# Filter rows and normed rows turned by DMA instead of TensorE in a fused SSM-convolution and SwiGLU kernel

## The chip, the cores and the metric

The kernel runs on one core of a Trainium2 chip. Its engines work in parallel: TensorE (PE, matrix products and transposes into PSUM), VectorE (DVE), ScalarE (ACT), GpSimd (POOL) and SyncE (SP), which issues nearly all DMAs. The metric is device time in microseconds of a whole execution; a kernel's figure is the median of several runs.

## The reference

The inputs are a sequence of S = 2048 rows with D = 576 columns, in bf16. Two residual branches follow each other, each behind a layer norm whose scale and shift come from a condition vector.

```python
mod = (silu(c) @ w_mod).reshape(1, 6, 1, -1)     # sa, ca, ga, sb, cb, gb
h = layernorm(x) * (1 + ca) + sa                 # x is A_q
# branch A: a short convolution of k by 4 taps, times v -> kv;
# then a long causal convolution along the sequence, by FFT of length 2S, with the filters ssm_k [D, S]
y = irfft(rfft(kv) * rfft(ssm_k).T)[:S] + kv * ssm_D
x = x + ga * (h * y)
# branch B: SwiGLU, w1 and w3 [576, 4608], w2 [4608, 576]
h = layernorm(x) * (1 + cb) + sb
x = x + gb * ((silu(h @ w1) * (h @ w3)) @ w2)
```

What matters below: the filters lie in DRAM with the channel as the row (ssm_k is [D, S]), while the convolution wants time on the partitions; and the normed rows of branch B have time on the partitions, while the products with w1 and w3 want the channel there. Both need a transpose.

## The kernel before, in words

**Tiling.** The sequence is cut into 8 blocks of B = 256 rows. A block is held as [128 partitions, 2, 576], where partition p holds rows 2p and 2p + 1. Branch A works block by block: the long convolution is done with the spectra of short blocks. For block s the filter's spectrum W (w_spectrum) gives V[s] (v_block), the spectrum of kv gives X[s] (x_spectrum), and the result of block s is the inverse of the sum of products X[i]·V[s - i] (pair, lines 412 to 425: VectorE's long products). X and V of earlier blocks are partly spilled to DRAM (keep_x, keep_v) and read back (get, line 442).

Branch B works on row blocks of RB = 512 rows, two convolution blocks each: stream(r) makes h3 = silu(h w1)·(h w3) for 36 column tiles of F, and down(r) multiplies it by w2, in two halves of 288 columns with nine chunks of w2 each. The last row block has its own stream_halves. w1 and w3 arrive in jobs of four column tiles (load_w13) in three buffers wst; in down the third of these holds a ring of four w2 chunks (NW2 = 4).

**Who makes whom wait.** While row block r goes through TensorE, the convolution of blocks 2r + 2 and 2r + 3 is computed beside it. conv(s0) is a generator of steps with a cost in microseconds at each yield. stream and down call advance after each piece of their own work, and advance runs steps until their costs have caught up (CONV_US, rate). So the convolution's TensorE work lies between the products of branch B, in an order fixed when the program is written out. end() runs all steps that are left. The instructions of each engine's queue are then ordered by a planner, which goes by dependencies and by its own estimate of when they are ready; `behind(engine)` pins the next instructions behind the last one written for that engine, and issue_after behind a named one. SP's queue is such a queue too: an instruction that waits there holds back all that follow.

**The filter rows.** load_k(s) (line 290) brings ssm_k[:, 256 s : 256 s + 256] into knat as five tiles of 128 channels by 256 times. k_rows(s) (line 368) transposes them on TensorE: ten transposes of 128x128 (line 376), five for the even and five for the odd times, into one PSUM buffer; ScalarE copies it to kT (line 378), the [128, 2, 576] form that w_spectrum multiplies (line 329). PSUM has four buffers of two banks for everything, one of which is taken here.

**The normed rows.** outcome(s) finishes a block: inverse (line 555), residual, then the statistics of the second norm on ScalarE (ln_sums, line 452), a few small VectorE and GpSimd instructions (ln_var, ln_shift), and the normed rows h2row, one buffer of [128, 2, 640], in which columns 512 to 576 stand twice (normed_act, line 582). turn_all(s) (line 794) turns h2row on TensorE with ten transposes (line 587), and `turned` (line 609) copies the result out of PSUM on ScalarE with scale and shift (1 + cb, sb) applied: five instructions of 128x256 (line 617) into h2T, of which there are two, one for each parity of the row block. For the even block of a pair turn_all is called inside the outcome of the odd block (`between`). For the odd block 2r + 3 it is called in down(r), in the second half behind chunk 7 of w2 (line 1088); chunk 8 follows, and then the first products of row block r + 1 (lines 967, or 1031 in the last row block) read h2T.

Block 0 and block 1 come first (first_block, conv_second), with row block 0 started on half of its rows.

Of the kernel before, what the change touches and what calls it, by code (L numbers as in the profile page):

```python
# [37 lines left out]
EPS = 1e-5  # L38

# [7 lines left out]
class _Kernel:  # L47
    def __init__(self, ctx, tc, q, k, v, shift_k, ssm_k, ssm_D, w1, w3, w2, c, w_mod, out):
        self.tc, self.nc = tc, tc.nc
        self.q, self.k, self.v = q, k, v  # L50
        self.shift_k, self.ssm_k, self.ssm_D = shift_k, ssm_k, ssm_D
        self.w1, self.w3, self.w2, self.c, self.w_mod, self.out = w1, w3, w2, c, w_mod, out
        pool = lambda name, **kw: ctx.enter_context(tc.tile_pool(name=name, **kw))
        self.const = pool("const", bufs=1)
        self.psum = pool("psum", bufs=4, space=bass.MemoryType.PSUM)
        self.dram = pool("spill", bufs=1, space=bass.MemoryType.DRAM)
        self.spec = pool("spec", bufs=4)
        self.wprev = pool("wprev", bufs=2)
        self.prod = pool("prod", bufs=1)
        self.acc = pool("acc", bufs=1)  # L60
        self.ld = pool("ld", bufs=1)
        self.kvp = pool("kvp", bufs=1)
        self.x1p = pool("x1p", bufs=4)
        self.lnp = pool("lnp", bufs=1)
        self.small = pool("small", bufs=4)
        self.hp = pool("hp", bufs=3)
        self.xo, self.hg, self.accs, self.l1 = {}, {}, {}, {}
        self.X, self.V, self.Wl = {}, {}, {}
        self.w13, self.kept = {}, {}

# [225 lines left out]

    def load_x(self, s):
        t = self.x1p.tile([P, 2, D], BF16, name="x1", tag="x1")
        self.nc.sync.dma_start(t[:], self.q[B * s:B * (s + 1), :].rearrange("(p c) d -> p c d", c=2))
        self.xo[s] = t  # L300
# [67 lines left out]
    def k_rows(self, s):  # L368
# [10 lines left out]
        if 2 < s < NBLK - 1:  # L379
            self.load_k(s + 1)  # L380
# [61 lines left out]
    def get(self, which, i):  # L442
        t = self.spec.tile([P, 6, D], BF16, name=which, tag=which, bufs=3 if which == "X" else 4)
        src = self.Xd if which == "X" else self.Vd
        self.nc.sync.dma_start(t[:].rearrange("p a d -> p (a d)"), src[i])
# [306 lines left out]
    def outcome(self, s, fill, waits, between=None, quick=False):  # L752


        def steps():
# [19 lines left out]
            else:  # L775
# [5 lines left out]
                yield -waits[2] / 2  # L781
                stats = self.ln_var(*sums, "l2")
# [11 lines left out]
    def turn_all(self, s):  # L794

        pt = self.ps((P, 2, 1024), BF16)
        for cc in range(2):
            self.turn(pt, cc)
        self.turned(s, pt, 0, 2)

    def conv_second(self):
        yield from self.gate_stats(1)
# [9 lines left out]
        self.load_k(2)  # L812
        yield from self.x_sums(1)
        yield from self.pair(self.X[1], self.V[0], 1)
# [4 lines left out]
    def conv(self, s0):  # L819
        s1 = s0 + 1  # L820
        if s0 == 2:
            self.load_k(s1)
# [4 lines left out]
        def filters():  # L827
            yield from self.k_rows(s1)
# [33 lines left out]
        def beside():  # L862
# [7 lines left out]
            yield from self.gate_stats(s1)  # L870
            if s0 > 2:
                yield from self.pair(X0, self.V[s0], s0)
# [5 lines left out]
            yield from self.pair(X0, self.V[s1], s1)  # L878
            self.gate_var(s1)
# [19 lines left out]
        if s1 + 1 < NBLK:  # L899
            with self.behind(self.nc.sync):  # L900
                self.load_kv(s1 + 1)
        yield from self.gate(s1)
        ahead = self.mix(self.filter_ahead(s1 + 1)) if s1 + 1 < NBLK else ()
        yield from self.outcome(s1, ahead, (5.0, 4.5, 5.0, 0.0), lambda: self.turn_all(s0))

    def filter_ahead(self, s):
        yield from self.k_rows(s)
        yield -4.0
        yield from self.w_spectrum(s)

# [156 lines left out]
    def down(self, r, rate):  # L1067
        nc = self.nc
        for h in range(2):
# [4 lines left out]
            for f0 in range(0, NF, W2C):  # L1074
# [3 lines left out]
                last = f0 + W2C == NF  # L1078
                order = [(f, t) for f in range(W2C) for t in range(4)]
# [8 lines left out]
                if h == 1 and f0 // W2C == 7 and r + 1 < NRB:  # L1088

                    self.end()  # L1090
                    self.turn_all(2 * r + 3)
                if (f0 // W2C) % 4 == 3:
# [132 lines left out]
```

## Time and profile before

| | us |
|---|---|
| median of 8 runs | 515.68 (514.29 to 516.08) |
| the profiled execution | 515.95 |
| its span in the trace | 514.2 |
| TensorE busy | 495.8 |
| VectorE busy | 337.5 |
| ScalarE busy | 294.7 |
| GpSimd busy | 27.1 |

The stages lie about so: the first block up to 35 us; row block 0 with blocks 1 to 3 up to 165, its down from 125; row block 1 up to 285, its down from 245; row block 2 up to 403, its down from 365; row block 3 to the end, its down from 474. TensorE's granted clock averages 0.993 over the span.

A row of a group reads: line, engine, operation, what it writes and reads, shape and count, then busy time, the mean of one in ns, and the idle time of the engine just before these instructions with what ended it. A row of a timeline begins with its start and its duration in us. A row of a window gives, for each engine, busy time and number of instructions, and at the end the granted clock, the mean busy share of the 16 DMA engines and GB/s.

### The profile page before, as it was taken

How to read it: one execution, taken by the hardware profiler on the slowest of the kernel's cores; microseconds unless marked ns; L12 is line 12 of the kernel's file. 1: busy time of each engine (PE TensorE's matmuls, PEld its weight loads, DVE VectorE, ACT ScalarE, POOL GpSimd, SP SyncE). 2: the span in 40 equal slices, each digit the busy share in tenths (PEclk: the TensorE clock that was granted, in tenths of full speed). 3: DMA queues.
4: the chain of work that ended last, by engine and by line, in shares of the span. 5: the costliest groups of instructions: out<-in, count | busy, mean ns of one | idle time of the engine just before them, and what ended most of it. 6: DMA issues, size and time to landing. Idle time of an engine off the chain costs nothing.

```text
span 514.2 us, 9042 instructions
## 1 busy us (share of the span) xinstructions
PE 495.8 (96%) x3630; PEld 299.8 (58%) x3650; DVE 337.5 (66%) x438; ACT 294.7 (57%) x581; POOL 27.1 (5%) x43
## 2 busy tenths in 40 slices
PE   6999999999999999999999999999999999999996
PEld 3667865457777444443787443434678555555774
DVE  8789899899889375999389995289761212112012
ACT  5749779769155679579352565975804555555000
POOL 4200001000001000000001000000000000000000
PEclk9979999999999999999999999999999999999999
DMA  8967869659989875387789594545554453460562
GB/s 259 285 205 208 278 205 300 189 180 320 323 274 324 277 217 170 104 293 270 210 266 290 166 321 155 171 108 170 160 143 113 149 174 113 165 183 3 139 169 62
DMA packets 101597, 104.25 MB, mean 203 GB/s; under 512 B 4979, under 2 KB 94132, under 8 KB 101556
## 3 DMA queue, kind: packets, MB, share of 16 engines
q1 hardware_dynamic: 101534, 103.68, 65.5%
q8 instruction: 28, 0.46, 0.4%
q14 instruction: 13, 0.11, 0.1%
q10 hardware_dynamic: 22, 0.01, 0.0%
HBM read 94.23 MB, written 9.44 MB: 202 GB/s over the span
## 4 chain that ended last, share of the span: by engine, by line
PE 67%; DVE 19%; DMA 4%; ACT 4%; issue 2%; POOL 2%; POOLq 0%; SPq 0%; DVEq 0%; ACTq 0%
PE ps L967 26%; PE ps L1085 16%; PE ps L1031 14%; DVE p L422 4%; PE ps L978 4%; DVE z L424 4%; DMA h<-in_w_mod_dram 2%; DMA kh<-in_A_k_dram 2%; PE ps L555 2%; PE ps L329 2%; DVE og L1107 1%; DVE h L992 1%; PE ps L315 1%; DVE kv L349 1%; POOL l2r L464 1%
## 5 line engine op out<-in xcount | busy, mean ns | idle before, releaser
L967 PE MATMUL ps<-h2T,wst 128*128 128x512 bf16 (+1 forms) x1037 | 198.9, 340 | 1.5 <-issue 0.3
L967 PEld LDWEIGHTS <-wst 128*128 128x128 bf16 x1056 | 100.0, 98 | 85.9 <-issue 14.6
L1085 PE MATMUL ps<-wst,h 128*128 128x288 bf16 x1152 | 146.0, 286 | 2.5 <-DMA wst<-in_B_w_dram 1.7
L1085 PEld LDWEIGHTS <-h 128*128 128x128 bf16 x1152 | 112.1, 98 | 32.7 <-issue 3.8
L985 ACT ACTIVATE h<-ps 128x512 bf16<-128x512 f32 x108 | 64.8, 600 | 63.3 <-PE ps L978 35.0
L1031 PE MATMUL ps<-h2T,wst 64*128 64x512 bf16 x648 | 70.3, 376 | 0.5 <-ACT h2T L617 0.5
L989 ACT CAST u<-ps 128x512 bf16<-128x512 f32 x108 | 63.3, 586 | 0.0
L1031 PEld LDWEIGHTS <-wst 64*128 64x128 bf16 x648 | 36.1, 94 | 34.1 <-issue 0.7
L422 DVE TENSOR_TENSOR p<-X,V 128x3456 bf16<-128x3456 bf16 x28 | 54.7, 1953 | 0.5
L424 DVE TENSOR_TENSOR z<-z,p 128x3456 bf16<-128x3456 bf16 x28 | 54.6, 1952 | 0.2
L1058 DVE TENSOR_TENSOR h<-h,u 128x1024 bf16<-128x1024 bf16 x18 | 12.4, 692 | 58.7 <-ACT u L1055 58.7
L992 DVE TENSOR_TENSOR h<-h,u 128x1024 bf16<-128x1024 bf16 x54 | 37.0, 684 | 17.2 <-ACT u L989 17.2
L1052 ACT ACTIVATE h<-ps 128x512 bf16<-128x512 f32 x36 | 21.5, 597 | 33.0 <-PE ps L1031 33.0
L452 ACT ACTIVATE junk<-x 128x576 bf16<-128x576 bf16 x54 | 37.2, 689 | 0.6
L1107 DVE TENSOR_TENSOR og<-ps,gbrow 128x576 bf16<-128x576 f32 (+1 forms) x18 | 12.3, 687 | 36.2 <-PE ps L1085 35.6
L978 PE MATMUL ps<-h2T,wst 64*128 64x512 bf16 (+1 forms) x264 | 33.1, 341 | 1.5 <-ACT u L989 1.2
L617 ACT ACTIVATE h2T<-ps,sbcol,cbcol 128x256 bf16<-128x256 bf16 x35 | 16.7, 570 | 17.7 <-PE ps L587 17.7
L978 PEld LDWEIGHTS <-wst 64*128 64x128 bf16 x264 | 8.5, 94 | 22.4 <-issue 20.9
L417 DVE TENSOR_TENSOR z<-X,V 128x3456 bf16<-128x3456 bf16 x7 | 13.7, 1953 | 11.8 <-PE ps L555 11.7
L1055 ACT CAST u<-ps 128x512 bf16<-128x512 f32 x36 | 20.9, 580 | 0.0
L582 ACT ACTIVATE h2row<-x,l2n,l2r 128x576 bf16<-128x576 bf16 (+1 forms) x24 | 13.7, 642 | 10.2 <-DVE l2n L470 10.0
L464 POOL TENSOR_TENSOR l2r<-l2v,neghalf 128x2 f32<-128x2 f32 x6 | 8.2, 1373 | 195.1 <-DVE l2v L460 195.1
(140 smaller groups left out, 401.5 us busy)
## 6 DMA issues: line engine op xcount, KB each, us to landing
wst<-in_B_w_dram SPq DMA_DIRECT2D x80, 512.0 KB, 4.3
wst<-in_B_w_dram SPq DMA_DIRECT2D x72, 288.0 KB, 3.1
wst<-in_B_w_dram SPq DMA_DIRECT2D x80, 64.0 KB, 3.4
kh<-in_A_k_dram SPq DMA_DIRECT2D x7, 720.0 KB, 6.7
X<-Xd SPq DMA_DIRECT2D x5, 864.0 KB
V<-Vd SPq DMA_DIRECT2D x5, 864.0 KB, 7.1
Xd<-X SPq DMA_DIRECT2D x4, 864.0 KB, 6.7
Vd<-V SPq DMA_DIRECT2D x4, 864.0 KB
```

Source lines behind the costliest of these rows:

```text
L422: nc.vector.tensor_mul(p[:], X[:], V[:])
L424: nc.vector.tensor_add(z[:], z[:], p[:])
L452: self.nc.scalar.activation(junk[:], src[:, i, :], func, scale=scale, accum_out=out[:, col:col + 1])
L967: nc.tensor.matmul(gus[k][:, i, a * n:(a + 1) * n], w[:, 5 * i + ct, (fi + a) * P:(fi + a + 1) * P], hT[:, ct, t0:t1], start=(first and ct ...
L978: nc.tensor.matmul(gus[k][:, i, a * n:(a + 1) * n], w[rows, 4, (fi + a) * P:(fi + a + 1) * P], hT[rows, 4, t0:t1], start=(first and a == 0 ...
L985: nc.scalar.activation(self.h3[:, f:f + m, t0:t1], gus[k][:, 0, :].rearrange("p (a t) -> p a t", a=m), ACT.Silu)
L989: nc.scalar.copy(self.u[:, k % 2, :], gus[k][:, 1, :])
L992: nc.vector.tensor_mul(h3, h3, self.u[:].rearrange("p b (a t) -> p (b a) t", a=m))
L1031: nc.tensor.matmul(gus[k][:, i, :], ws[fc][rows, 5 * i + ct if ct < 4 else 4, cols], hT[rows, ct, :], start=swap == 0 and ct == 4, stop=sw ...
L1052: nc.scalar.activation(h3, gus[k][:, 0, :], ACT.Silu)
L1055: nc.scalar.copy(self.u[:, k % 2, :], gus.pop(k)[:, 1, :])
L1085: nc.tensor.matmul(acc[t], self.h3[:, f0 + f, t * P:(t + 1) * P], w[:, f, :], start=(f0 + f == 0), stop=(f0 + f == NF - 1))
```

## The change

For blocks 2 to 7, TensorE no longer transposes. load_taps(s) reads the filters with a transposing DMA from DRAM into knat, which then holds the times 0 to 127 and 128 to 255 on the partitions. pair_taps(s) copies from there to kT in four DMAs inside SBUF, which bring even and odd times together. k_rows remains for blocks 0 and 1 alone. turn_all(s) issues two transposing DMAs from h2row to h2T for s > 1, and modulate(s) applies scale and shift in h2T in place: on ScalarE within outcome and for block 3, on VectorE for blocks 5 and 7. load_taps(s + 1) is written where the filters of block s are done with, pair_taps in down behind turn_all for odd blocks and behind load_kv for even ones. All of these DMAs are in SP's queue. Two orders change beside it: reads of spilled X and V (get) are pinned behind the last w2 load of down's first half, and for s0 = 2 the statistics of the first norm of block 3 come after the products of X[0].

```diff
@@ -36,6 +36,8 @@
 HEAD_PACE = 1.4
 AHEAD = 2
 EPS = 1e-5
+TURN = 7
+QUICK = False
 
 
 def _ap(t, offset, dims):
@@ -67,6 +69,7 @@
         self.xo, self.hg, self.accs, self.l1 = {}, {}, {}, {}
         self.X, self.V, self.Wl = {}, {}, {}
         self.w13, self.kept = {}, {}
+        self.last_w2 = None
 
     def newest(self):
         return self.nc.cur_bb.bb.instructions[-1]
@@ -294,6 +297,21 @@
                         self.ssm_k[0:512, B * s:B * (s + 1)].rearrange("(a p) t -> p a t", p=P))
         queue.dma_start(t[0:64, 4, :], self.ssm_k[512:D, B * s:B * (s + 1)])
 
+    def load_taps(self, s):
+
+        nc = self.nc
+        nc.sync.dma_start_transpose(_ap(self.knat, 0, [[D, 2], [1, D]]), self.ssm_k[:, B * s:B * (s + 1)])
+
+    def pair_taps(self, s):
+
+        nc = self.nc
+        self.kT = self.kvp.tile([P, 2, D], BF16, name="kT", tag="kT")
+        taps = self.knat[:].rearrange("p a b -> p (a b)")
+        for half in range(2):
+            for cc in range(2):
+                nc.sync.dma_start(self.kT[64 * half:64 * half + 64, cc, :],
+                                  taps[cc:P:2, half * D:(half + 1) * D])
+
     def load_x(self, s):
         t = self.x1p.tile([P, 2, D], BF16, name="x1", tag="x1")
         self.nc.sync.dma_start(t[:], self.q[B * s:B * (s + 1), :].rearrange("(p c) d -> p c d", c=2))
@@ -376,8 +394,6 @@
                 nc.tensor.transpose(pt[:, cc, ct * P:(ct + 1) * P], nat[:, ct, cc:B:2],
                                     self.ident[:])
         nc.scalar.copy(kT[:], pt[:, :, 0:D])
-        if 2 < s < NBLK - 1:
-            self.load_k(s + 1)
         self.kT = kT
         yield 0.2
 
@@ -442,7 +458,8 @@
     def get(self, which, i):
         t = self.spec.tile([P, 6, D], BF16, name=which, tag=which, bufs=3 if which == "X" else 4)
         src = self.Xd if which == "X" else self.Vd
-        self.nc.sync.dma_start(t[:].rearrange("p a d -> p (a d)"), src[i])
+        with self.tc.issue_after(self.last_w2) if self.last_w2 is not None else nullcontext():
+            self.nc.sync.dma_start(t[:].rearrange("p a d -> p (a d)"), src[i])
         return t
 
     def ln_sums(self, src, i, ssum, ssq, col=None):
@@ -749,7 +766,7 @@
             if d >= 0:
                 yield d
 
-    def outcome(self, s, fill, waits, between=None, quick=False):
+    def outcome(self, s, fill, waits, between=None, then=None, quick=False):
 
 
         def steps():
@@ -779,6 +796,8 @@
                         self.ln_sums(self.xo[s], i, *sums)
                     yield 0.0
                 yield -waits[2] / 2
+                if then is not None:
+                    then()
                 stats = self.ln_var(*sums, "l2")
                 yield -waits[2] / 2
                 scales = self.ln_shift(*stats)
@@ -793,12 +812,31 @@
 
     def turn_all(self, s):
 
+        if s > 1:
+            hT = self.h2T[(s // 2) % 2]
+            for cc in range(2):
+                t = 2 * (s % 2) + cc
+                self.nc.sync.dma_start_transpose(hT[:, :, t * P:(t + 1) * P], self.h2row[:, cc, :])
+            return
         pt = self.ps((P, 2, 1024), BF16)
         for cc in range(2):
             self.turn(pt, cc)
         self.turned(s, pt, 0, 2)
 
+    def modulate(self, s, quick):
+
+        part = self.h2T[(s // 2) % 2][:, :, 2 * (s % 2) * P:2 * (s % 2 + 1) * P]
+        for ct in range(5):
+            x, scale, bias = part[:, ct, :], self.cbcol[:, ct:ct + 1], self.sbcol[:, ct:ct + 1]
+            if quick:
+                self.nc.vector.tensor_scalar(x, x, scale, bias, op0=ALU.mult, op1=ALU.add)
+            else:
+                self.nc.scalar.activation(x, x, ACT.Identity, bias=bias, scale=scale)
+
     def conv_second(self):
+        with self.behind(self.nc.sync):
+            self.load_taps(2)
+            self.pair_taps(2)
         yield from self.gate_stats(1)
         yield from self.kv_rows(1)
         yield from self.v_block(1)
@@ -809,8 +847,9 @@
         self.mod_piece(5)
         self.gate_rows(1)
         yield from self.gate(1)
-        self.load_k(2)
         yield from self.x_sums(1)
+        with self.behind(self.nc.sync):
+            self.load_taps(3)
         yield from self.pair(self.X[1], self.V[0], 1)
         yield from self.outcome(1, self.mix(self.filter_ahead(2)), (5.0, 3.5, 0.0, 2.0), quick=True)
         self.turn_all(1)
@@ -819,13 +858,13 @@
     def conv(self, s0):
         s1 = s0 + 1
         if s0 == 2:
-            self.load_k(s1)
+            with self.behind(self.nc.sync):
+                self.pair_taps(s1)
         else:
             self.load_x(s0)
             self.load_x(s1)
 
         def filters():
-            yield from self.k_rows(s1)
             yield -4.0
             yield from self.v_block(s0)
             yield from self.w_spectrum(s1)
@@ -867,8 +906,10 @@
             self.gate_shift(s0)
             with self.behind(self.nc.sync):
                 self.load_kv(s1)
-            yield from self.gate_stats(s1)
+                if s1 + 1 < NBLK:
+                    self.load_taps(s1 + 1)
             if s0 > 2:
+                yield from self.gate_stats(s1)
                 yield from self.pair(X0, self.V[s0], s0)
             if s0 < NBLK - 2:
                 self.X1 = self.old_x(1, s0)
@@ -876,6 +917,8 @@
                 self.V1 = self.old_v(1, s0)
             self.gate_rows(s0)
             yield from self.pair(X0, self.V[s1], s1)
+            if s0 == 2:
+                yield from self.gate_stats(s1)
             self.gate_var(s1)
             yield from self.gate(s0)
         yield from self.mix(self.x_spectrum(s0), beside())
@@ -899,14 +942,18 @@
         if s1 + 1 < NBLK:
             with self.behind(self.nc.sync):
                 self.load_kv(s1 + 1)
+                self.pair_taps(s1 + 1)
         yield from self.gate(s1)
         ahead = self.mix(self.filter_ahead(s1 + 1)) if s1 + 1 < NBLK else ()
-        yield from self.outcome(s1, ahead, (5.0, 4.5, 5.0, 0.0), lambda: self.turn_all(s0))
+        yield from self.outcome(s1, ahead, (5.0, 4.5, 5.0, 0.0), lambda: self.turn_all(s0),
+                                lambda: self.modulate(s0, QUICK))
 
     def filter_ahead(self, s):
-        yield from self.k_rows(s)
         yield -4.0
         yield from self.w_spectrum(s)
+        if 2 < s < NBLK - 1:
+            with self.behind(self.nc.sync):
+                self.load_taps(s + 1)
 
 
     def load_w13(self, fc, buf):
@@ -1076,6 +1123,8 @@
                 nc.sync.dma_start(w, self.w2[f0 * P:(f0 + W2C) * P, h * H:(h + 1) * H]
                                   .rearrange("(a p) d -> p a d", p=P))
                 last = f0 + W2C == NF
+                if h == 0 and last:
+                    self.last_w2 = self.newest()
                 order = [(f, t) for f in range(W2C) for t in range(4)]
                 if f0 == 0:
                     order = [(f, t) for t0 in (0, 2) for f in range(W2C) for t in (t0, t0 + 1)]
@@ -1085,10 +1134,13 @@
                     nc.tensor.matmul(acc[t],
                                      self.h3[:, f0 + f, t * P:(t + 1) * P], w[:, f, :],
                                      start=(f0 + f == 0), stop=(f0 + f == NF - 1))
-                if h == 1 and f0 // W2C == 7 and r + 1 < NRB:
+                if h == 1 and f0 // W2C == TURN and r + 1 < NRB:
 
                     self.end()
                     self.turn_all(2 * r + 3)
+                    if 2 * r + 5 < NBLK:
+                        self.pair_taps(2 * r + 5)
+                    self.modulate(2 * r + 3, r > 0)
                 if (f0 // W2C) % 4 == 3:
 
                     leave = ((self.keep_v, 3), (self.keep_v, 2), (self.keep_x, 2), (self.keep_x, 3)) if r == 0 else ()
```

## The prediction

> **What bounds the kernel now.** I read the engine rows of the page first, then the groups by shape, TensorE's timeline around each transpose, and last the DMA share stage by stage.
>
> ```profile
> PE 495.8 (96%) x3630; PEld 299.8 (58%) x3650; DVE 337.5 (66%) x438; ACT 294.7 (57%) x581; POOL 27.1 (5%) x43
> DMA  8967869659989875387789594545554453460562
> ```
>
> TensorE works through 96% of the span, so time taken off it can come off the end. The DMA row shows the other limit: its first half stands at 5 to 9, its second mostly at 4 or 5.
>
> Groups by shape (count, busy us, mean ns, idle before):
>
> ```profile
> L376 PE MATMUL ps<-ident,knat 128*128 128x128 bf16 x80 | 6.3, 231 | 3.1 <-POOL knat L661 1.5 <-DVE og L1107 1.1 <-DMA knat<-in_A_ssm_k_dram 0.6
> L587 PE MATMUL ps<-ident,h2row 128*128 128x128 bf16 x70 | 5.4, 220 | 0.5 <-ACT h2row L582 0.5
> L378 ACT COPY kT<-ps 128x1152 bf16<-128x1152 bf16 x8 | 8.9, 1118 | 14.3 <-PE ps L376 14.2
> ```
>
> Transposes overlap in TensorE, so 231 ns is not what one costs. The timeline (start, duration) tells that:
>
> ```profile
> 150.04 0.72 PE L587 MATMUL ps<-ident,h2row 128*128 128x128 bf16 x10
> 150.60 8.00 PE L1085 MATMUL ps<-wst,h 128*128 128x288 bf16 x64
> ...
> 399.21 0.56 PE L587 MATMUL ps<-ident,h2row 128*128 128x128 bf16 x5
> 400.30 0.56 PE L587 MATMUL ps<-ident,h2row 128*128 128x128 bf16 x5 [0.53 <-ACT h2row L582]
> 400.70 2.12 PE L1085 MATMUL ps<-wst,h 128*128 128x288 bf16 x16
> ```
>
> Ten transposes hold TensorE for 150.60 - 150.04 = 0.56 us. The last set also waits for its rows: 400.70 - 399.21 = 1.5 us.
>
> **What is removed.** For blocks 2 to 7 one set of ten in k_rows and one in turn_all: 12 sets. Eleven at 0.56 make 6.2 us, the last 1.5; beside them the set at 71.37 waited 0.61 for knat, and the first L1031 at 403.33 waited 0.51 for h2T. Sum: 8.8 us, by stage: 3.4 up to 165.4 (blocks 2, 3, filter rows of 4), 2.2 from there to 285.4, 3.2 after it. ScalarE loses six copies of kT at 1.12 (6.7 us), which are off the path: it is idle 43%. The 0.77 and 0.29 us that sets at 168.70 and 288.07 waited for og stay: they are waits for a PSUM buffer, and the next user of that buffer inherits them.
>
> **What is added.** Per block: one transpose of 288 KB from DRAM (load_taps) in place of two loads of the same bytes; four copies inside SBUF of 72 KB each (pair_taps); two transposes of 160 KB (turn_all); five instructions of 128x256 on ScalarE or VectorE (modulate) in place of five that read PSUM. So 608 KB more per block, 3.6 MB on 104, and five DMA issues more on SP.
>
> modulate: L617's 128x256 from PSUM advances 2.39/5 = 0.48 us each; I take the same in SBUF. On VectorE the nearest row is L487's (295 ns for 64 columns, 427 for 576), about 0.34 for 256, so 1.7 us for five.
>
> The transposes themselves have no row. Lower bound: they move like copies, 320 KB at the 319 GB/s of a busy stage (shown below), 1.0 us for a turn and 0.9 for a load_taps. The Trainium skill has two prices. "Advanced Engine Details and Errata", section "X-Bar Transpose (TRN2)", puts them near regular DMAs, 350 to 400 GB/s: the same 1 us. "VectorE: DVE Perf Modes", section "The three transpose paths", gives 1309 ns for one 128x128 by DMA against 390 on TensorE, and its rules prefer TensorE when PSUM will do. The trace's TensorE figure is 0.056 per tile, so the alternative is cheaper here than the page's own. Ten tiles in series at 1.309 would be 13.1 us a turn, nine for a load_taps 11.8. That is the upper bound. I take 2.5 us for either, nearer the copy, whose loads of 128 partitions keep the DMA share at 0.97[...], but not at its price.
>
> **Where it meets the path.** Three turns matter, those of blocks 3, 5 and 7: each feeds the next row block's first matmul, one w2 chunk (2.1 us) later. DMA by stage (last two columns are share and GB/s):
>
> ```profile
> 120.00:165.00 45.00, 44.22 (x381) 35.07 (x379) 40.00 (x47) 22.75 (x47) 3.46 (x2) 1.00 0.97 319
> 245.00:288.00 43.00, 41.43 (x345) 32.12 (x344) 31.62 (x31) 16.23 (x32) 2.33 (x1) 1.00 0.80 252
> 365.00:403.00 38.00, 37.03 (x309) 29.16 (x308) 16.47 (x25) 17.13 (x38) 1.38 (x2) 1.00 0.54 149
> ```
>
> *Block 3 (row block 0 to 1).* DMA is full, and what is issued lands late; between 150 and 175 us:
>
> ```profile
> wst<-in_B_w_dram SPq DMA_DIRECT2D x3, 512.0 KB, 6.7
> wst<-in_B_w_dram SPq DMA_DIRECT2D x4, 288.0 KB, 5.8
> ```
>
> ScalarE's h2row and h2T there:
>
> ```profile
> 159.90 2.29 ACT L582 ACTIVATE h2row<-x,l2n,l2r 128x576 bf16<-128x576 bf16 x4 [3.62 <-DVE l2n L470]
> 163.73 2.39 ACT L617 ACTIVATE h2T<-ps,sbcol,cbcol 128x256 bf16<-128x256 bf16 x5 [1.54 <-PE ps L587]
> ```
>
> Rows are complete at 162.2, h2T at 166.1. By DMA they stand behind kh and w13: 5.8 us to landing (the smallest neighbour) is 168.0, and with 2.4 of modulate 170.4. The first half-sum needs four column tiles, so 170.0 where TensorE had them by its own fourth matmul at about 166.3: 3.7 late. What was saved ahead of the inverse at 142.3 (k_rows of 2, 3, 4 and the 0.61: 2.3 us) can bring the rows forward, so 1.4 to 3.7 late; I take 2.5. With transposes slower than copies (2.5 against 1.0) it is 4.0 late at the start of row block 1, although 3.4 had been saved.
>
> *Block 5 (1 to 2).* Rows are ready at 275.85, TensorE wants h2T at 285.4: ten microseconds cover a landing of 7. But the last w2 chunk already arrives 1.30 late, and turn plus pair_taps put 608 KB, 1.9 us, into the same queue; 1.5 more for the slower transposes; and VectorE, busy without a gap from 268.8, gets 1.7 us of modulate ahead of the og that frees PSUM. These overlap: I count 3.4 of loss against 2.2 of saving, +1.2.
>
> *Block 7 (2 to 3).* DMA has room. And a wait falls away: ScalarE stood 5.75 us for block 6's transposes before L617 at 391.56, with block 7's statistics behind it in order, from 393.82, though x was ready at 387.4. With turn_all off TensorE they start at once, rows come some 5 us before 400.6, and even 6 us of transpose are hidden until chunk 8 ends. The whole 3.2 is gained. If that cover fails, a landing of 5 us after 400.6 plus 1.7 gives 407.3 against 403.3.
>
> *SP's order.* pair_taps follows load_taps by a block, except at block 2, where it waits for the landing while w13 loads stand behind it; the next w13 load went out at 39.40, ten microseconds after SP's last issue at 29.02, which hides it. Between w2 loads (ring of four: three chunks, 6.1 us, less 3.1 to landing) six more issues at about 0.5 fill the slack of 3 without much over: +0.5 in all. If a transpose held SP for 2 us each, w13 and w2 behind it would be the next to be late.
>
> Sum against the profiled execution (515.95: span 514.2 and 1.75 around it): +4.0 + 1.2 - 3.2 + 0.5 = +2.5, 518.45; the median stands 0.27 below that execution, so **518.2 us**.
>
> **Rivals.**
> *The transposes are as quick as copies and the rows come early (faster).* Then block 3 ends 0.5 late instead of 4.0, block 5 keeps 1.2 of its 2.2, block 7 all: +0.5 - 1.2 - 3.2 = -3.9 with SP's part hidden: 511.8. For it: TensorE's 96%, and saving spread over every stage. Against: the 0.97 share just where block 3 turns. The sign is decided by issue to landing of block 3's transposes: 3.5 us or less keeps a gain, 5.8 loses it.
> *The page's serial price (much slower).* Turns of 13 us: block 3 about 8 late net, block 5 (275.85 + 13.1 + 1.7 against 285.4, with 2.2 saved) 3, block 7 (395.5 + 13.1 + 1.7 against 403.3) 7, SP blocked in between: 515.7 + 18 = 534.
> *The two sides cancel:* TensorE shortens but VectorE (40.0 busy of 45 up to 165) and PSUM release set the stage ends; 515.7.
>
> **How the numbers follow.** Chances: the forecast 0.43, quick transposes 0.41, serial price 0.10, cancelled 0.06. The forecast's own range is 516.8 to 522. For eight in ten I leave out about a quarter of the quick case below 509.5 and most of the serial one above 528. A measurement of this kernel tells 0.2%, 1.0 us, from no change: faster 0.41, same 0.06, slower 0.53.
>
> **What would show it.** No L376 after 30 us and no L587 after 66. Rows of block 3 to their landing 5 us or more, L967 near 165 waiting for h2T by some 4 us; at 3 us or less the forecast is wrong and the first rival right. The last w2 chunk before row block 2 waits for DMA 2 us or more. Block 7's statistics directly after its residual, and L1031 without a wait. SP's transposes longer than 1 us each in issue would move stalls into w2 loads, which I count small.

## The result, and the profile after

The changed kernel takes 509.97 us (median of 11 runs, 508.83 to 515.62) beside 515.62 for the kernel before in the same series. The ratio is 0.9902, 95% interval 0.9883 to 0.9921: faster by 1%, where a slower kernel was forecast. The profiled execution has a span of 508.1 us against 514.2. The chips of the series below differ a little, so kernels are compared by their ratio to the kernel before on the same chip; 0.001 of ratio is 0.5 us.

The engine row and the DMA row of the changed kernel's page:

```profile
PE 489.4 (96%) x3510; PEld 287.9 (57%) x3530; DVE 339.7 (67%) x448; ACT 283.8 (56%) x565; POOL 24.8 (5%) x43
DMA  8998987759999894448799996745474554560562
```

TensorE is busy 6.4 us less, about the span's 6.1. The DMA row is fuller than before: by the pages, the packets of its queue took 71.8% of the 16 engines' time, and 65.5% before.

What TensorE waits for has changed too. Groups of the kernel after: w2 products (L1134), w1 and w3 products of the last row block (L1078), the new work on h2T, and the issues of the transposes:

```profile
L1134 PE MATMUL ps<-wst,h 128*128 128x288 bf16 x1152 | 145.4, 286 | 4.7 <-DMA wst<-in_B_w_dram 3.5
L1078 PE MATMUL ps<-h2T,wst 64*128 64x512 bf16 x648 | 70.3, 376 | 0.0
L834 ACT ACTIVATE h2T<-h2T,sbcol,cbcol 128x256 bf16<-128x256 bf16 x20 | 10.4, 589 | 18.5 <-DMA h2T<-h2row 18.5
L832 DVE TENSOR_SCALAR h2T<-h2T,cbcol,sbcol 128x256 bf16<-128x256 bf16 x10 | 2.7, 342 | 5.2 <-DMA h2T<-h2row 5.2
h2T<-h2row SPq DMA_TRANSPOSE x12, 4.2
knat<-in_A_ssm_k_dram SPq DMA_TRANSPOSE x6, 5.1
```

The wait for w2 grew from 1.7 to 3.5 us, the wait of L1078's forerunner L1031 for h2T (0.5) is gone, and the transposes take 4 to 5 us (median) from issue to landing.

**Block 3, into row block 1.** Here the forecast put its largest loss. ScalarE's timeline in the changed kernel (four statistics passes, the rows, scale and shift), and TensorE's:

```profile
147.86 0.69 ACT L469 ACTIVATE junk<-x 128x576 bf16<-128x576 bf16 x1
...
155.74 2.29 ACT L599 ACTIVATE h2row<-x,l2n,l2r 128x576 bf16<-128x576 bf16 x4 [4.67 <-DVE l2n L487]
163.25 2.56 ACT L834 ACTIVATE h2T<-h2T,sbcol,cbcol 128x256 bf16<-128x256 bf16 x5 [5.22 <-DMA h2T<-h2row]
```

```profile
151.60 2.12 PE L1134 MATMUL ps<-wst,h 128*128 128x288 bf16 x16 [0.39 <-DMA wst<-in_B_w_dram]
155.69 8.00 PE L1134 MATMUL ps<-wst,h 128*128 128x288 bf16 x64 [1.98 <-DMA wst<-in_B_w_dram]
163.90 0.38 PE L1014 MATMUL ps<-h2T,wst 128*128 128x512 bf16 x1 [0.20 <-ACT h2T L834]
164.17 2.12 PE L1134 MATMUL ps<-wst,h 128*128 128x288 bf16 x16
166.12 1.67 PE L1014 MATMUL ps<-h2T,wst 128*128 128x512 bf16 x6
```

The rows are complete at 155.74 + 2.29 = 158.03, the transposes land at 163.25, and h2T is done at 165.81, where it was 166.12 before. TensorE waits 0.20 us for it. What it does wait for is w2: 0.39 and 1.98 us, before any row of block 3 is turned. The statistics begin at 147.86 and not at 153.06, as they did in the kernel before, whose ScalarE had this order:

```profile
150.80 2.39 ACT L617 ACTIVATE h2T<-ps,sbcol,cbcol 128x256 bf16<-128x256 bf16 x5 [1.88 <-PE ps L587]
153.06 0.70 ACT L452 ACTIVATE junk<-x 128x576 bf16<-128x576 bf16 x1
```

There the copies of block 2's transposes out of PSUM (L617) stood ahead of block 3's statistics and waited for TensorE, which had w2 products in its own queue first. The statistics waited with them.

**Block 7, into row block 3.** TensorE and VectorE after:

```profile
385.72 9.47 PE L1134 MATMUL ps<-wst,h 128*128 128x288 bf16 x76
395.40 2.12 PE L1134 MATMUL ps<-wst,h 128*128 128x288 bf16 x16 [0.21 <-DMA wst<-in_B_w_dram]
397.46 10.75 PE L1078 MATMUL ps<-h2T,wst 64*128 64x512 bf16 x98
```

```profile
393.48 1.37 DVE L832 TENSOR_SCALAR h2T<-h2T,cbcol,sbcol 128x256 bf16<-128x256 bf16 x5 [5.19 <-DMA h2T<-h2row]
```

The h2T of block 7 is ready at 394.85, 2.6 us before TensorE asks for it.

**Where the 6.1 us lie.** The first products of row blocks 1, 2 and 3 start as follows (for row block 1 the run of matmuls behind the last w2 chunk):

| | before | after | gained in the stretch |
|---|---|---|---|
| row block 1 | 165.50 | 166.12 | -0.6 |
| row block 2 | 285.36 | 282.28 | 3.7 |
| row block 3 | 403.33 | 397.46 | 2.8 |
| end of the span | 514.2 | 508.1 | 0.2 |

The transposes removed are shared out by the forecast as 3.4, 2.2 and 3.2. Up to row block 1 all of it is lost again, and 0.6 us more: 4.0 us. Of these the waits for w2 explain 1.9 (2.37 for 0.45). The rest lies in waits of 0.4 to 1.1 us for ScalarE and VectorE between 73 and 132 us, which no run takes apart. Behind row block 1 the gain is more than what was removed, by the 0.77 and 0.29 us that TensorE had waited for og at 168.70 and 288.07, which are gone, and by w2: in row block 1's down projection it is waited for 0.34 + 0.53 = 0.87 us, and 1.30 before.

### The profile page after: what moved, and what is told of

Read it like the earlier page. It is cut to its first block, busy times and chain, and to the rows that moved or that the text cites. A ratio compares the mean times of both kernels' runs of the same rounds, so it can differ in the third digit from the quotient of the medians.

```text
span 508.1 us, 8853 instructions
## 1 busy us (share of the span) xinstructions
PE 489.4 (96%) x3510; PEld 287.9 (57%) x3530; DVE 339.7 (67%) x448; ACT 283.8 (56%) x565; POOL 24.8 (5%) x43
## 2 busy tenths in 40 slices
DMA packets 115036, 107.97 MB, mean 213 GB/s; under 512 B 20339, under 2 KB 107572, under 8 KB 114996
## 3 DMA queue, kind: packets, MB, share of 16 engines
q1 hardware_dynamic: 114974, 107.41, 71.8%
## 4 chain that ended last, share of the span: by engine, by line
PE 63%; DVE 18%; DMA 8%; ACT 5%; issue 3%; POOL 1%; SPq 1%; POOLq 0%; DVEq 0%; ACTq 0%
PE ps L1014 24%; PE ps L1134 15%; PE ps L1078 14%; PE ps L1025 4%; DVE p L438 3%; DMA kh<-in_A_k_dram 3%; DMA V<-Vd 2%; DVE z L440 2%; PE ps L333 2%; DVE h L1039 2%; DVE z L433 2%; DVE og L1159 1%; PE ps L347 1%; ACT junk L469 1%; DMA wst<-in_B_w_dram 1%
## 5 line engine op out<-in xcount | busy, mean ns | idle before, releaser
L1134 PE MATMUL ps<-wst,h 128*128 128x288 bf16 x1152 | 145.4, 286 | 4.7 <-DMA wst<-in_B_w_dram 3.5
L1134 PEld LDWEIGHTS <-h 128*128 128x128 bf16 x1152 | 112.4, 98 | 36.3 <-issue 6.2
L1078 PE MATMUL ps<-h2T,wst 64*128 64x512 bf16 x648 | 70.3, 376 | 0.0
L1078 PEld LDWEIGHTS <-wst 64*128 64x128 bf16 x648 | 31.1, 94 | 38.6 <-DVE og L1159 0.2
L834 ACT ACTIVATE h2T<-h2T,sbcol,cbcol 128x256 bf16<-128x256 bf16 x20 | 10.4, 589 | 18.5 <-DMA h2T<-h2row 18.5
L1025 PEld LDWEIGHTS <-wst 64*128 64x128 bf16 x264 | 8.5, 94 | 21.5 <-issue 18.7
L367 DVE TENSOR_TENSOR kv<-kv,p 128x1152 bf16<-128x1152 bf16 x24 | 18.1, 752 | 0.3
L361 DVE TENSOR_TENSOR p<-kh,shk 128x3456 bf16<-128x3456 bf16 x8 | 15.6, 1951 | 1.0 <-ACT dcol L676 0.6
```

Source lines behind the costliest of these rows:

```text
L1025: nc.tensor.matmul(gus[k][:, i, a * n:(a + 1) * n], w[rows, 4, (fi + a) * P:(fi + a + 1) * P], hT[rows, 4, t0:t1], start=(first and a == 0 ...
L1078: nc.tensor.matmul(gus[k][:, i, :], ws[fc][rows, 5 * i + ct if ct < 4 else 4, cols], hT[rows, ct, :], start=swap == 0 and ct == 4, stop=sw ...
L1134: nc.tensor.matmul(acc[t], self.h3[:, f0 + f, t * P:(t + 1) * P], w[:, f, :], start=(f0 + f == 0), stop=(f0 + f == NF - 1))
```

## The experiments

The theory after the result had three parts: TensorE gains the time of its transposes; ScalarE's queue is rid of a wait that held the statistics back; and the price is paid in w2 loads that come late, where DMA is full. The rivals say that the gain is in one part alone (the filters, or the normed rows), that it is in an order that the change altered beside the transposes, or that late rows are what costs.

**One part alone.** First the normed rows by DMA with the filter rows on TensorE (`e1_turns_only`), and the reverse (`e2_taps_only`). Both keep the two changes of order.

```diff
 # e1_turns_only, against the kernel after
-            self.load_taps(2); self.pair_taps(2)     # and the other calls of both
+        self.load_k(2)                               # and the other calls of load_k
+        yield from self.k_rows(s1)                   # and in filter_ahead
 # e2_taps_only, against the kernel after
-        if s > 1:
+        if False:
             hT = self.h2T[(s // 2) % 2]
...
-                                lambda: self.modulate(s0, QUICK))
+                                None)
...
-                    self.modulate(2 * r + 3, r > 0)
```

> Normed rows by DMA, filter rows on TensorE as before. Theory (the turns unblock ScalarE: the odd block's statistics no longer queue behind the even block's PSUM copies, and the late w2 loads come from the kT copies): most of the gain stays, about 4.5 us, near 511.1; rows of block 3 complete about 4 us and of block 5 about 9 us earlier than before; the 2 us wait for w2 near 155 us is gone. Rival (only TensorE's removed time counts, the same for each of the twelve sets): half of the gain, 2.8 us, near 512.8.

> Filter rows by DMA, normed rows on TensorE with scale and shift on the way out of PSUM, as before. Theory: 6 x 0.56 + 0.6 = 4.0 us of TensorE saved, less 2 to 3 us of late w2 loads, nothing unblocked: about 1 us faster than before, near 514.6. Rival (each set counts the same): half of the gain, 2.8 us, near 512.8.

Measured: e1 517.34 us, ratio 1.0009 (0.9990 to 1.0028), no gain at all; e2 512.05, 0.9910 (0.9880 to 0.9940). Both expectations for e1 were missed; e2 was better than its theory's 514.6 and near its rival's 512.8. The filters alone, with both changes of order, bring 0.9%, 4.6 us. Six sets of 0.56, the 0.61 for knat and the two waits for og of 0.77 and 0.29 are gone in e2: 5.0 us. The changed kernel has only 0.08% more than e2 (-0.28 to 0.44), so a gain from the normed rows on top of the filters is not shown: the 4.8 us that their transposes took from TensorE were lost again but for 0.4 us (at most 2.3).

**The two orders.** e1 gained nothing, so the places of the gate statistics and of the reads of X and V were put back: in e6 both, with the normed rows by DMA and the filters on TensorE; in e5 the gate statistics alone, with all of the rest changed.

```diff
 # e5_old_stats_place and e6_turns_plain
+            yield from self.gate_stats(s1)
             if s0 > 2:
-                yield from self.gate_stats(s1)
                 yield from self.pair(X0, self.V[s0], s0)
...
-            if s0 == 2:
-                yield from self.gate_stats(s1)
             self.gate_var(s1)
 # e6_turns_plain alone, with the filter rows as in e1
-        with self.tc.issue_after(self.last_w2) if self.last_w2 is not None else nullcontext():
+        if True:
             self.nc.sync.dma_start(t[:]
```

> The changed kernel, with block 3's first-norm statistics back in their old place, ahead of the products of X[0]. Theory A (the new place costs row block 0 about 1 us: waits of 0.39 and 0.64 at 105 and 108 us that the kernel before has not): about 1 us faster than the changed kernel, 509.0. Theory B (the new place takes away the wait of 1.2 us at 92 us and is worth it): about 1 us slower, 511.

> Only the normed rows turned by DMA: filter rows on TensorE, block 3's statistics and the reads of spilled X and V placed as in the kernel before. Theory A (turns by themselves gain, and the run with turns only lost it to the two changes of order): 2 to 3 us faster than before, 513. Theory B (turns gain nothing: TensorE's 3 us go to w2 loads that stand behind transposes on SP and to the DMA time of the transposes): 515.5 to 516.5, with waits of TensorE for w2 of 3 us or more.

Measured: e5 511.38, 0.9894 (0.9862 to 0.9927), no different from the changed kernel, so neither of its two theories is borne out; e6 513.88, 0.9957 (0.9937 to 0.9977). So the gain is not in the place of the gate statistics. The normed rows alone do bring 0.4%, 2.2 us, if the two orders are left as they were; the orders cost a kernel with the filters on TensorE 0.5%. In e6 five sets of 0.56, the 1.5 and the 0.51 are removed, and the two waits for og (1.06) are gone as well: 5.9 us, of which 3.7 are lost. Its profile says to what. TensorE's waits in e6 and in the kernel before (waiting line and what it waited for; us in total, times, longest):

```profile
PE ps L1125 <- DMA wst<-in_B_w_dram: 5.1, 6, 1.4
PE ps L1005 <- DMA wst<-in_B_w_dram: 0.6, 1, 0.6
```

```profile
PE ps L1085 <- DMA wst<-in_B_w_dram: 1.7, 2, 1.3
PE ps L376 <- DVE og L1107: 1.1, 2, 0.8
```

That is 5.7 against 1.7 us: 4 us more of waits for weights, nearly all w2, about what went missing. The gains of e2 and e6 add to 1.3% (0.9 to 1.7), the changed kernel has 1.0% (0.8 to 1.2). So the parts may simply add, or the second may add nothing to the first; these runs do not tell the two apart.

**ScalarE's queue alone.** The kernel before, with the even block's turn_all moved behind the odd block's statistics; all transposes stay on TensorE.

```diff
 # e3_stats_first, against the kernel before
                     yield 0.0
                 yield -waits[2] / 2
+                if then is not None:
+                    then()
...
-        yield from self.outcome(s1, ahead, (5.0, 4.5, 5.0, 0.0), lambda: self.turn_all(s0))
+        yield from self.outcome(s1, ahead, (5.0, 4.5, 5.0, 0.0), None, lambda: self.turn_all(s0))
```

> The kernel before with all its transposes on TensorE; only the even block's turn (transposes and PSUM copies) is written after the odd block's statistics. Theory of the unblocking: rows of block 7 complete about 5 us earlier, TensorE no longer waits for them (0.53, the rest of the 1.5, and 0.51): 1.4 us faster than before, near 514.2. Rival (the order on ScalarE is worth nothing, it had slack): 515.6, and rows of blocks 3, 5 and 7 complete as before.

Measured: 514.38 us, 0.9974 (0.9959 to 0.9989), the theory's number. ScalarE in it, block 3:

```profile
149.33 0.69 ACT L452 ACTIVATE junk<-x 128x576 bf16<-128x576 bf16 x1
...
154.42 2.40 ACT L617 ACTIVATE h2T<-ps,sbcol,cbcol 128x256 bf16<-128x256 bf16 x5 [2.69 <-PE ps L587]
156.69 2.30 ACT L582 ACTIVATE h2row<-x,l2n,l2r 128x576 bf16<-128x576 bf16 x4
```

The rows are complete at 156.69 + 2.30 = 158.99, 3.2 us earlier than before, without a transpose moved; for block 5 it is 5.8 and for block 7 3.2 us. That this wait in the queue held the rows back is shown. The edit is worth 0.26%, some 1.3 us, but not where the theory put it, so the agreement of the number is luck. By the starts of the row blocks (165.85, 283.70, 401.65) e3 gains 2.0 us between row blocks 1 and 2, where the 1.30 for w2 and the 0.77 for og are gone, and nothing between 2 and 3: there the last set takes 0.9 us less, but TensorE waits 0.9 more for og at 287.30, and it still waits 0.53 for h2T. That earlier rows gave the 1.3 us is not shown. With the filters by DMA as well (`e8_taps_stats_first`, e2 with the same move) it should have come on top:

> Filter rows by DMA, normed rows on TensorE, the even block's turn after the odd block's statistics. If the gains of the run with filter rows only (0.9%) and of the run with statistics first (0.26%) add up: 1.15% faster than before, near 509.8, as fast as the changed kernel without any turn by DMA. If the turns by DMA do something that neither has: slower than the changed kernel by 1 us or more, 511 to 512.

Measured: 512.93, 0.9930 (0.9908 to 0.9951). It did not come on top: by its ratio e8 is 1.4 us slower than the changed kernel, the second expectation, and not told apart from e2. In its profile TensorE waits 2.7 us for og in front of a w2 product, which e2 does not. So early rows by themselves gained nothing beside the filters here; what they would be worth without that wait is not shown.

**Are late rows the price?** In e7 four passes of 128x576 that nobody reads stand on ScalarE ahead of the odd block's statistics.

```diff
 # e7_rows_later, against the kernel after
+            if then is not None:
+                for _ in range(4):
+                    with self.behind(nc.scalar):
+                        junk = self.lnp.tile([P, D], BF16, name="junk", tag="junk")
+                        nc.scalar.activation(junk[:], self.xo[s][:, 0, :], ACT.Copy)
```

> The changed kernel with four idle passes over x on ScalarE (4 x about 0.65 = 2.6 us) ahead of the odd block's second-norm statistics, their output unused. Theory (block 3's rows are on the path with no slack, blocks 5 and 7 have 8 and 3 us): rows of block 3 come 2.6 us later and TensorE stands that long before row block 1, +2 to +2.6, near 512.3; nothing at the other two boundaries. Rival (rows are early everywhere, the gain is TensorE's removed work alone): no difference, 510.

Measured: 511.40, 0.9907 (0.9871 to 0.9943), by its ratio nearer the rival. ScalarE in it:

```profile
147.84 2.83 ACT L788 ACTIVATE junk<-x 128x576 bf16<-128x576 bf16 x4
...
157.06 2.29 ACT L599 ACTIVATE h2row<-x,l2n,l2r 128x576 bf16<-128x576 bf16 x4 [3.16 <-DVE l2n L487]
162.91 2.57 ACT L839 ACTIVATE h2T<-h2T,sbcol,cbcol 128x256 bf16<-128x256 bf16 x5 [3.57 <-DMA h2T<-h2row]
```

The rows are complete at 159.35, 1.3 us later than in the changed kernel, yet scale and shift start 0.3 us earlier: the transposes took 3.3 us from issue to landing (median) for 4.5 in the changed kernel. So at block 3 the landing did not follow the rows over this range; that DMA's other traffic sets it is likely, and not shown. TensorE does wait 1.04 us for w2 at 164.98, for a load that SyncE issued behind the transposes 0.9 us later than in the changed kernel; but e5, without the idle passes, has 0.81 there too. At block 7, where DMA has room, the delay does reach TensorE, which waits 0.69 us for h2T in this kernel. The interval just reaches the theory's 2 us, so the theory is not excluded.

**Where the price is paid.** In e4 the copies of pair_taps for blocks 5 and 7 were written in the next conv and not in down, to keep them out from between the w2 loads.

```diff
 # e4_pair_late, against the kernel after
-                    if 2 * r + 5 < NBLK:
-                        self.pair_taps(2 * r + 5)
...
 # at the start of conv(s0), for s0 > 2
+            with self.behind(self.nc.sync):
+                self.pair_taps(s1)
```

> The changed kernel, but the kT copies of blocks 5 and 7 are issued at the start of the next row block instead of between the w2 loads of down. Theory: the late w2 loads near 151 and 155 us (0.39 + 1.98) and some of the 0.87 near 264 to 276 go, 1.5 to 2.5 us faster than the changed kernel, near 508. Rival (DMA is full there whatever, 0.97 of it): same as the changed kernel, 510, w2 as late as before. If the copies arrive late for the filter's spectrum, slower.

Measured: 509.88, 0.9874 (0.9841 to 0.9907), not told apart from the changed kernel. It settles nothing: in the trace SyncE still issued copies of kT at 152 to 156 us between the w2 loads, so what the edit was to move had not moved, and TensorE still waited 1.98 us there.

Then the normed rows by DMA in some blocks only, the others on TensorE and the filters by DMA in both: in g1 blocks 4 to 7, in g4 blocks 2 and 3.

```diff
 # g1_turns_late_only; in g4_turns_early_only 1 < s < 4, s0 < 4 and r == 0
-        if s > 1:
+        if s > 3:
             hT = self.h2T[(s // 2) % 2]
...
-                                lambda: self.modulate(s0, QUICK))
+                                (lambda: self.modulate(s0, QUICK)) if s0 > 3 else None)
...
-                    self.modulate(2 * r + 3, r > 0)
+                    if r > 0:
+                        self.modulate(2 * r + 3, r > 0)
```

> The changed kernel, but blocks 2 and 3 have their normed rows transposed on TensorE as before; blocks 4 to 7 and all filters stay on DMA. Theory (the transposes' price is DMA time, and it is paid only where the queues are full, around row block 0's second half of the down projection, where w2 chunks of 0.39 and 1.98 us are waited for near 152 to 156 us): these waits fall back to the 0.5 us of the kernel before, TensorE takes 2 sets x 0.56 = 1.1 us back, net about 1 us faster than the changed kernel, 508.5 to 509. Rival (the queue is full everywhere and the waits only move, as they did when one part was taken out before): the same 510 or up to 1.1 us slower, 510 to 511.

> The changed kernel, but only blocks 2 and 3 are transposed by DMA; blocks 4 to 7 go back to TensorE, filters stay on DMA. Theory (the gain of the transposes sits in the two later row blocks, the cost in the first): no better than the filters alone (512.05), so 512 to 513. Rival (each set gives its 0.56 us and unblocks ScalarE wherever it is): a third of the way from 512.05 to 509.97, about 511.3.

Measured: g1 510.45, 0.9895 (0.9871 to 0.9919); g4 513.93, 0.9957 (0.9936 to 0.9979). By the differences of the ratios, blocks 2 and 3 by DMA are worth +0.47% (0.10 to 0.84) added to e2, so slower, and +0.07% (-0.24 to 0.38) added to g1; blocks 4 to 7 bring 0.55% (0.26 to 0.84) added to g4, but only 0.15% (-0.23 to 0.53) added to e2. The theory for g4 holds in so far as blocks 2 and 3 by themselves do not pay; that the later ones do is seen beside blocks 2 and 3 alone. For g1 the wait went as the theory said, but no time came with it. TensorE's waits for w2 in g4 and g1:

```profile
PE ps L1134 <- DMA wst<-in_B_w_dram: 5.9, 5, 2.0
```

```profile
PE ps L1134 <- DMA wst<-in_B_w_dram: 2.5, 6, 0.8
```

The wait of about 2 us at 155 to 156 us is in the changed kernel, e4, e5, e7 and g4, all with block 2's rows and the filters by DMA; where one of the two is on TensorE (e1, e2, e6, e8, g1, g3, g5) there are 0.6 us or less. SyncE's queue in the changed kernel and in g1 shows what is ahead of those w2 loads (L1123):

```profile
126.55 2.33 SPq L1123 DMA_DIRECT2D wst<-in_B_w_dram  x2
128.97 2.79 SPq L819 DMA_TRANSPOSE h2T<-h2row  x2
...
147.07 4.53 SPq L1123 DMA_DIRECT2D wst<-in_B_w_dram  x3
151.66 1.82 SPq L312 DMA_DIRECT2D kT<-knat  x2
```

```profile
126.44 2.29 SPq L1123 DMA_DIRECT2D wst<-in_B_w_dram  x2
128.78 0.51 SPq L966 DMA_DIRECT2D wst<-in_B_w_dram  x1
...
147.60 2.57 SPq L1123 DMA_DIRECT2D wst<-in_B_w_dram  x2
150.27 0.63 SPq L312 DMA_DIRECT2D kT<-knat  x1
```

One pair of transposes holds SyncE for 2.79 us at 128.97, and some twenty microseconds later three w2 loads take 4.53 us to issue, with the copies of kT behind them. That the one leads to the other is argued from their order, not shown.

**Order of issue, or DMA time?** In g3 the last w2 chunk is loaded ahead of the odd block's transposes, in e6's kernel; in g5 the same for blocks 5 and 7, in g1's.

```diff
 # g3_w2_ahead_of_turn, against e6_turns_plain
                     self.end()
-                    self.turn_all(2 * r + 3)
+                    ws[f0 + W2C] = load(f0 + W2C)     # the chunk's dma_start, not issued again later
+                    with self.behind(nc.sync):
+                        self.turn_all(2 * r + 3)
```

> Normed rows by DMA, filters on TensorE, old places of the gate statistics and of the state loads (513.88 us without this edit), and in addition the last w2 chunk's load is written ahead of the odd block's transposes, which are pinned behind it in SyncE's queue. Theory (the w2 waits of 0.79 at 284 and 1.44 at 400 us come from that load being issued 2.5 us late behind two transposes): these two go, about 2 us, 511.9. Rival (it is the transposes' DMA time, whatever the order of issue): the waits stay or turn into a wait for the turned rows, 513.5 to 514.5.

> The changed kernel with two edits that each took TensorE's waits for w2 away somewhere: blocks 2 and 3 transposed on TensorE as before (510.45 us alone), and for blocks 5 and 7 the last w2 chunk's load written ahead of the two transposes. Theory (the order of issue in SyncE's queue costs time wherever a w2 load stands behind two transposes): the 0.76 and 0.25 us of w2 waits left at 281 and 396 us go, about 1 us, 509.4, so at or just under the changed kernel's 509.97. Rival (with the filters on DMA these waits do not decide): no difference, 510 to 511.

Measured: g3 512.15, 0.9928 (0.9905 to 0.9952), against 0.9957 for e6: about 1.5 us better, near the theory, though the intervals overlap. SyncE and TensorE of e6 at block 7:

```profile
392.97 2.53 SPq L821 DMA_TRANSPOSE h2T<-h2row  x2
395.59 0.53 SPq L1114 DMA_DIRECT2D wst<-in_B_w_dram  x1
```

```profile
400.03 2.12 PE L1125 MATMUL ps<-wst,h 128*128 128x288 bf16 x16 [1.44 <-DMA wst<-in_B_w_dram]
```

And of g3:

```profile
387.96 4.29 SPq L1116 DMA_DIRECT2D wst<-in_B_w_dram  x3
392.30 2.53 SPq L821 DMA_TRANSPOSE h2T<-h2row  x2
```

```profile
387.77 11.92 PE L1133 MATMUL ps<-wst,h 128*128 128x288 bf16 x96
```

In e6 the w2 load stood behind the two transposes for their 2.53 us of issue, and TensorE waited 1.44 us for it; in g3 TensorE goes through. So at block 7, where DMA has room, the price is SyncE's issue time: the same transposes, issued behind the load, cost TensorE nothing there. At block 5 it is not: g3 still waits 1.8 and 0.6 us near 280. And g5 gave 510.28, 0.9877 (0.9854 to 0.9899), the rival's value, not told apart from g1 or from the changed kernel. Its profile has a wait of 3.35 us for w2 at 280.62, although the load was issued ahead of the transposes. No version here beats the changed kernel by more than can be measured.

## Why the prediction was wrong

The prediction set 11.3 us of losses against 8.8 saved. Measured were 9.9 us saved (the 8.8, and 1.06 of og waits) and a gain of 6.1, so 3.8 of losses. **The steps that failed are block 3, +4.0 us, and block 5, +1.2**: of the 8.6 us between the forecast for the span (+2.5) and its -6.1, they make 3.4 and 4.9. Behind both stands one wait, in ScalarE's queue, that the prediction counted for block 7 alone.

**Block 3** measured +0.6. The prediction took the rows at 162.2 us, brought forward by at most the 2.3 us saved ahead of the inverse, and had h2T late by what the transposes take longer. The rows came 4.2 us earlier (162.19 to 158.03), because block 3's statistics no longer stood behind block 2's copies out of PSUM; e3 gives 3.2 of it to this queue alone. The prediction described just this for block 7 and put it at nothing for blocks 3 and 5; the same two rows, L617 and L452, were in the trace at 150.80 and 153.06. The landing was put too long as well: 5.8 us and 1.5 more for slow transposes, where 5.2 was measured (158.03 to 163.25). Only modulate was right, 2.56 for 2.4. And the other side of the comparison moved: TensorE came to row block 1 0.6 us later than before, having lost 4.0 us against 3.4 saved, 1.9 of them to waits for w2, so that h2T, 0.3 us earlier than before, cost 0.20. That rows 3.2 us later would have cost TensorE about that is worked out from this trace; e7 held them up by 1.3 us alone.

**Block 5 had the wrong sign:** the stretch gained 3.7. Rows were complete at 266.42, not 275.85, with ScalarE's queue again the larger part (5.8 us in e3). Scale and shift on VectorE (272.56 to 273.93) lay long before the og at 283.36, so nothing waited for it. The late w2 chunk did not get later: SyncE issued the transposes from 266.58 on and the last chunk at 273.94, when they had landed, and TensorE did not wait for it; the waits in that down projection were 0.87 us for 1.30. The 3.4 us of losses that the step counted were not found; the rest of the miss is the og waits. SyncE in the changed kernel:

```profile
266.58 2.78 SPq L819 DMA_TRANSPOSE h2T<-h2row  x2
...
273.94 0.37 SPq L1123 DMA_DIRECT2D wst<-in_B_w_dram  x1
```

**The og waits "stay" was wrong.** Both (1.06 us), at 168.70 and 288.07, are gone in the changed kernel and in e2. They are gone in e6 too, where those sets stay on TensorE, while e3 and e1, which also keep them, wait up to 1.2 and 1.4 us; e8, without the sets, waits 2.7 us for og at a w2 product. So these waits hang on the order in each kernel; why they went is not shown.

**Right in mechanism and near in size:** block 7 (-3.2 forecast, -2.8 measured), with the statistics directly behind the residual and L1078 without a wait; 0.34 us for each of modulate's instructions on VectorE; the TensorE time removed.

**SyncE, +0.5 us, was too small.** The text named a transpose that holds SyncE for 2 us as what would shift stalls into w2 loads. It was 1.2 us for each normed-row transpose and 1.3 to 2.9 for a filter one, and more stalls were seen there: the changed kernel waits 1.7 us more for w2 than the kernel before, all of it and more ahead of row block 1 (2.37 for 0.45). Whether SyncE's time or DMA's makes them in that stage is not shown.

**Of the rivals,** the first ended nearest (511.8), by half of its reason. The rows did come early. But it asked for quick transposes as well, and named 3.5 us from issue to landing at block 3 as the most that keeps a gain; the landing there took 4.5 us in the median and the gain was kept. With rows 4.2 us earlier, h2T was in time at that landing.

**What stays open.** Why the waits for w2 near 280 us come and go was not separated: 0.5 us in e2 and 2.8 in g4, which do the same there, 1.7 in g1 and 3.35 in g5; so a single wait of that stage is no evidence. That blocks 2 and 3 by DMA cost time beside e2 and none beside g1 lies at the edge of the intervals. The two altered orders were not taken apart in e1; only the gate statistics were tried alone, in the full kernel. No run has the filters by DMA with the reads of X and V in their old place, so the share of that order in e2's 0.9% is not known. The profiled executions of e4, e7, e8, g4 and g5 were the longest of theirs, 1.6 to 3.1 us over the median, so a wait in one of these traces need not be in the others.

## What to carry to other kernels

When work leaves an engine, look at every instruction that stood behind its consumers in an in-order queue: a copy out of PSUM waiting for a busy TensorE held back statistics that needed nothing from it, at each of three blocks and not only where the longest wait showed. Earlier rows are time only where something waited for them: moving that copy alone brought the rows forward by 3.2 to 5.8 us and the kernel by 1.3. Price a DMA transpose by what stands behind it in its issuing queue as well as by its landing: a load that is due soon goes ahead of it (g3 gained at block 7 by this; in g5 it made no difference). And compare arrival with the need in the changed timeline, since both ends move.

## What the runs showed of the hardware

A transpose of 128x640 in bf16 inside SBUF holds SyncE for 1.23 us (median of twelve, 1.22 to 1.60), and one from DRAM into 128 partitions of 2x576 for 1.3 to 2.9, where the w2 load at 395.59 took 0.53. From issue to landing the first takes 2.6 us at block 7 and up to 4.6 where DMA is full. In the Trainium skill, "VectorE: DVE Perf Modes", section "The three transpose paths", has 1309 ns for one 128x128 by DMA, of which the prediction made 13.1 us for a turn in series as its upper bound; the whole turn of ten tiles at block 7 took 3.9 us, from the first issue at 389.55 to scale and shift at 393.48.

In DMA time they look dearer than copies all the same. The window from 130 to 140 us, before and then after (last three columns: clock, DMA share, GB/s):

```profile
130.00:140.00 10.00, 9.66 (x84) 7.49 (x83) 10.00 (x9) 1.12 (x1) 0.00 (x0) 1.00 1.08 328
```

```profile
130.00:140.00 10.00, 9.15 (x76) 7.07 (x75) 9.97 (x10) 2.99 (x6) 0.00 (x0) 1.00 1.19 241
```

By their share the engines are as full, but they move 0.87 MB less in ten microseconds. If the turn and the filter transpose issued at 129 to 134 us (608 KB) all fall in it, they took the time in which 0.62 + 0.87 = 1.49 MB go at 328 GB/s, 4.5 us: an estimate of 140 GB/s that takes all else in both windows to run alike, between the two prices of the prediction and near its 2.5 us each. Packets under 512 bytes went from 4979 to 20339, which fits. The share is not even: of quarter-microsecond slices of this window the one from 134.75 to 135.0 counts 9.12, and in the 1.75 us behind it DMA moved 40 GB/s or less. The kernel before has no such stretch there. That the transposes are its cause is read from their place, not shown.
